# Weight tiles of one mode instead of two, with six of their real parts loaded as 40 and 24 rows

## The chip, the core and the metric

The kernel runs on one core of one Trainium2 chip. Its time is the device time of one execution, in microseconds (us), and the figure that is compared is the median over runs. The core has TensorE (PE), VectorE (DVE), ScalarE (ACT), GpSimd (POOL) and SyncE (SP), each with its own instruction order, and 16 DMA engines which the transfers of all queues share.

## The reference

Inputs are q, k, v of shape (8, 8, 576, 64) (batch, head, position, width), spectral weights `w_r` and `w_i` of shape (64, 512, 512) and `w_ch` of shape (512, 512), all fp32. The weights `w_r` and `w_i` are 64 MB of fp32 each.

```python
scores = (q @ k.transpose(0, 1, 3, 2)) / sqrt(64)
rel = pos[:, None] - pos[None, :]
local   = (rel >= 0) & (rel < 32)                       # heads 0 to 3
strided = (rel >= 0) & (pos[None] % 32 == pos[:, None] % 32)  # heads 4 to 7
x = softmax(where(mask, scores, -1e9)) @ v              # (8, 576, 512) over all heads
X = rfft(x, axis=1)[:, :64]                             # 64 modes
Yr = Xr @ w_r[m] - Xi @ w_i[m]                          # for each mode m
Yi = Xr @ w_i[m] + Xi @ w_r[m]
u = x + irfft(Y, n=576, axis=1)
out = u + relu(u @ w_ch)
```

## The kernel before

**Stages.** The order of work on every engine is written out by hand. First comes the strided attention (heads 4 to 7) batch by batch, a loop `for b in range(B)` in which the front work of the next batch (transposes of its q, k and v) is woven into the scores of this one; each batch ends with its share of the forward transform, so that the spectrum `Xh[1]` is complete after it. Then the local attention (heads 0 to 3) runs batch by batch, and between its steps lie the products of "slot 0": for all 64 modes, the half of the channels that the strided heads gave. `NMODES` says how many modes go with each batch. When the local heads are done, `Xh[0]` is complete and "slot 1" follows: for all 64 modes the other half of the channels. Between those modes lie other pieces from a list `work` (`w_turn`, which folds the inverse transform's turn into the channel weights, then `turn` and `premix` of each batch) and `spec`, which carries finished groups of 16 modes back; for the last ten modes of the loop (`LATE = 10`, modes 51 to 60) the list gives two pieces a mode. Modes 61 to 63 are done among the first steps of the tail. The tail adds the inverse transform's last group, takes the relu (`v_rows`), adds it to u (`u_rows`) and writes the output in 512 KB transfers.

**One mode.** `mode(slot, m)` does 16 matmuls (line 547) of a 128x128 piece of the weight tile with a 128x16 piece of the spectrum. The tile has the real part of the weights in partitions 0 to 63 and the imaginary part in 64 to 127, so one product sums both. Mode 0 has no imaginary part in its input and uses 64 partitions.

**Weights.** `w_fetch` (line 174) issues the loads of a tile on GpSimd's queue; the transfer turns fp32 into fp16, so an 8 KB row in DRAM becomes 4 KB in a partition. A tile holds two consecutive modes: 8 KB in each of 128 partitions. Its real part is one transfer of 64 partitions by two modes (line 196), 512 KB as written, and its imaginary part is another. The last four modes, and the imaginary part of the tiles with mode 0, go mode by mode (line 199), 256 KB each. Tiles come from a pool `pw` with five buffers (`NWBUF = 5`), apart from three pairs, `GUEST`, which lie in the places of the spectra `Y0`, `X0` and `YT` before these are needed. `mode` calls `w_fetch` after each odd mode, so that a buffer that has just been read is asked for again; the first stage fetches ahead:

```python
        w_fetch([2, 1, 1, 1, 1, 1, 0, 0][b])
```

which with one tile before the loop makes eight pairs, 16 modes.

**Inputs of the attention.** `load_str(b, nb)` brings v, q and k of the strided heads into `ring`, a store of 12 slots of 2048 fp16, three slots to a batch. A batch's input is 72 rows of 32 positions by 64: rows 0 to 63 are one transfer (for `nb == 2`, one transfer for the two batches of an even and odd pair), and rows 64 to 71 of both batches of a pair are one more transfer of eight rows by two (64 KB). `load_loc` brings the local heads' q, k and v, 128 rows each, 288 KB.

**Queue.** GpSimd issues all these in the order of the program, and waits ahead of an issue until the buffer is free and until the transfer eight places earlier has landed: there are eight semaphores for its transfers, used in turn. GpSimd's other work lies in the tail, where it adds x to the relu (line 905).

**Tiles of the tail.** `w_ch` has a place of its own in `big`. The relu's output `rl` takes two tags, `xT` and `rl`, with two buffers each in the pool `ptr`; the output tiles `osb` take slots of `pw`, free once the last weights have been used.

Of the kernel before, what the change touches and what calls it, by code (L numbers as in the profile page):

```python
# [10 lines left out]
FP = mybir.dt.float32  # L11
F16 = mybir.dt.float16
# [6 lines left out]
DM = 512  # L19
NM = 64  # L20
# [3 lines left out]
JG = [(0, 6), (6, 11), (11, 16)]  # L24
SCALE = float(1.0 / np.sqrt(D))
NEG = -30000.0
NWBUF = 5


def _host_consts():  # L30
# [49 lines left out]
def kernel(  # L80
# [10 lines left out]
    nc = tc.nc  # L91
# [3 lines left out]
    big = ctx.enter_context(tc.tile_pool(name="big", bufs=1))  # L95
# [5 lines left out]
    def psum_pools(**bufs):  # L101
        pctx.close()
        for n, c in bufs.items():
            pss[n] = pctx.enter_context(
                tc.tile_pool(name="ps_" + n, bufs=c, space=PSUM)
            )

    def psum(kind, half=False):
        if half:
            return pss[kind].tile([128, 1024], F16, tag=kind, name=kind)  # L110
        return pss[kind].tile([128, 512], FP, tag=kind, name=kind)
# [16 lines left out]
    def const_load(eng, *which):  # L128
        for n in which:
            eng.dma_start(cs[n][:, 0 : hosts[names.index(n)].shape[1]], drams[n])  # L130
# [13 lines left out]
    def spectra_tile(n):  # L144
        if n == "X0":
            Xh[0] = big.tile([128, 4, B, 2, NM], F16, tag=n, name=n)
        else:
            YS[n] = big.tile([128, 4, 4, 16, 16], F16, tag=n, name=n)

    xb = [px.tile([128, 11, 256], F16, tag="xb", name="xb") for _ in range(B)]  # L150

    pw = ctx.enter_context(tc.tile_pool(name="pw", bufs=NWBUF))
    actx = ctx.enter_context(ExitStack())
# [3 lines left out]
    ring = pat.tile([128, 12, 2048], F16, name="ring")  # L157
# [8 lines left out]

    GUEST = {1: "Y0", 2: "X0", 7: "YT"}
    w_tiles = []  # L170
    w_chs = {}
    w_ch = big.tile([128, 4, DM], F16, name="w_ch")

    def w_fetch(n=1):
        for _ in range(n):
            i = len(w_tiles)
            if i >= 2 * NM:
                return
            half, m = 1 - i // NM, i % NM
            if i // 2 in GUEST:  # L180
                wt = big.tile([128, 2, 4, DM], F16, tag=GUEST[i // 2], name="wt")
            else:
                wt = pw.tile([128, 2, 4, DM], F16, tag="w", name="wt")
            for ri, src in enumerate((moe_w_r, moe_w_i)):
                dst = wt[ds(64 * ri, 64)]
                rows = src[m : m + 2, ds(256 * half, 256), :].rearrange(
                    "m (p c) e -> p m (c e)", c=4
                )
                dst = dst.rearrange("p m c e -> p m (c e)")


                ones = range(2)
                if ri and not m:
                    ones = [1]
                elif i < 2 * NM - 4:
                    nc.gpsimd.dma_start(dst, rows)  # L196
                    continue
                for j in ones:
                    nc.gpsimd.dma_start(dst[:, j], rows[:, j])
            w_tiles.extend((wt[:, 0], wt[:, 1]))  # L200

    def w_ch_fetch():
        nc.gpsimd.dma_start(w_ch, moe_w_ch.rearrange("(c p) e -> p c e", p=128))
        w_chs["n"] = w_ch

# [3 lines left out]
    SRC = {2: v, 0: q, 1: k}  # L209
    SLOT = {2: 0, 0: 1, 1: 2}  # L210

    def str_in(b, vi):
        return ring[0:72, 3 * (b % 4) + SLOT[vi], :]
# [2 lines left out]
        t = ring[:, ds(2 * (b % 6), 2), :].rearrange("p n x -> p (n x)")  # L216
        return t[:, ds(1152 * vi, 1152)]

    def load_str(b, nb):
        for vi in (2, 0, 1):  # L220
            n = 3 * (b % 4) + SLOT[vi]
            two = ring[:, n : n + 4 : 3, :]
            src = SRC[vi][b - b % 2 : b - b % 2 + 2, 4:8].rearrange(
                "b h (c r) d -> (h c) b (r d)", r=32
            )
            if nb == 2:
                nc.gpsimd.dma_start(two[0:64], src[0:64])
            else:
                nc.gpsimd.dma_start(ring[0:64, n, :], src[0:64, b % 2])
            if b % 2 == 0:  # L230
                nc.gpsimd.dma_start(two[64:72], src[64:72])

    def load_loc(*bs):
        for b in bs:
            if b >= B:
                return
            for vi in (2, 0, 1):
                nc.gpsimd.dma_start(
                    loc_in(b, vi),
                    SRC[vi][b, 0:4].rearrange("h (cb i) d -> (h cb) (i d)", i=18),  # L240
                )
# [294 lines left out]
    def mode(slot, m):  # L536
        half = 1 - slot
        mi, mg = m % 8, m // 8
        if mi == 0:
            ypt[slot] = psum("y")  # L540
        yp = ypt[slot]
        yv = yp.rearrange("p (m e x) -> p m e x", m=8, e=4)
        wt = w_tiles[slot * NM + m]
        pr = ds(0, 128 if m else 64)
        for e in range(4):
            for c in range(4):
                nc.tensor.matmul(  # L547
                    yv[:, mi, e, :],
                    wt[pr, XC[c], ds(128 * e, 128)],
                    Xh[half][pr, c, :, :, m],  # L550
                    start=(c == 0),
                    stop=(c == 3),
                )
        if m % 2 and (slot or m // 2 not in GUEST):
            w_fetch()
        ends = {7: 8}
        if slot and mg == 7:
            ends = {5: 6, 7: 2}
        if mi in ends:
            n = ends[mi]  # L560
            m0 = mi + 1 - n
            part = (
                slice(None),
                slice(None),
                mg // 2,
                slice(None),
                ds(8 * (mg % 2) + m0, n),
            )
            src = yp.rearrange("p (m e x) -> p e x m", m=8, e=4)[:, :, :, ds(m0, n)]
            if slot == 0:  # L570
                if m == 7:
                    spectra_tile("Y0")
                nc.scalar.activation(out=YS["Y0"][part], in_=src, func=ACTF.Copy)
            else:
                nc.vector.tensor_tensor(
                    out=YS["YT"][part], in0=src, in1=YS["Y0"][part], op=AluOp.add
                )
# [117 lines left out]


    psum_pools(tp=3, sc=3, av=2)
    load_str(0, 1)
    const_load(nc.scalar, "cI", "cM6", "cM5", "cFs")
    load_str(1, 1)  # L700
    const_load(nc.sync, "cMl", "cFl", "cA")
    load_str(2, 2)
    w_fetch()

    def str_front(b):
        return [
            lambda: str_v(b, 0), lambda: str_v(b, 1),
            lambda: str_v(b, 2), lambda: str_q(b, 0),
            lambda: str_back(b, 0),
            lambda: str_back(b, 1), lambda: str_q(b, 1),  # L710
            lambda: str_k(b, 0),
            lambda: str_k(b, 1), lambda: str_k(b, 2),
        ]
# [29 lines left out]
                )  # L743
    SPLIT = [0, 2, 4, 5, 7, 8, 10]
    for b in range(B):
        if b in (1, 3):
            load_str(b + 3, 2)
        load_loc(*[(), (), (), (), (0,), (1, 2), (3,), (4, 5)][b])
        w_fetch([2, 1, 1, 1, 1, 1, 0, 0][b])
        front = str_front(b + 1) if b + 1 < B else loc_front(0)  # L750
        for t in range(6):
            str_scores(b, t)
            if b > 0:
                if t < 2:
                    str_values(b - 1, 4 + t)
                elif t == 2:
                    dft(b - 1, 1)
            if t >= 2:
                str_values(b, t - 2)
            for w in front[SPLIT[t] : SPLIT[t + 1]]:  # L760
                w()
        if b == 1:
            nc.vector.memset(PL[:, 0:PS0], 0.0)
# [10 lines left out]
    for b in range(B):  # L774
# [12 lines left out]
        n = 0  # L787
        nm = NMODES[b]
        for mi in range(nm):
# [3 lines left out]
            n = upto  # L793
# [5 lines left out]
    ptr = ctx.enter_context(tc.tile_pool(name="ptr", bufs=1))  # L799
# [37 lines left out]
    n = 0  # L837
# [3 lines left out]
    for m in range(NM - 3):  # L841
# [7 lines left out]
        n = upto  # L849
# [11 lines left out]
    held, vps, ups, rls, osbs = {}, {}, {}, {}, {}  # L861
# [24 lines left out]
    def v_early(i, bank=None):  # L886
        b, t = units[i]
        vps[i] = psum("v") if bank is None else bank
        v0 = v0s[b][:, t, :] if t < 4 else v0h[b // 2]
        nc.tensor.matmul(vps[i], idn, v0, start=True, stop=False)  # L890

    def v_rows(i):
        b, t = units[i]
        if i not in vps:
            v_early(i)
        vp = vps.pop(i)
        rows_of(b, t, vp, zzs, False)
        if t % 2 == 0:
            n = len(rls) // 2 % 2
            rl = ptr.tile([128, 2, 576], FP, tag="xT" if n else "rl", bufs=2, name="rl")  # L900
            rls[b, t] = rls[b, t + 1] = rl[:, :, 0:DM]
        rl = rls[b, t][:, t % 2, :]
        nc.scalar.activation(out=rl, in_=vp, func=ACTF.Relu)  # L903
        if pool_adds(b, t):
            nc.gpsimd.tensor_tensor(out=rl, in0=rl, in1=x_rows(b, t), op=AluOp.add)  # L905
# [56 lines left out]
    for i in range(len(units)):  # L962
        v_rows(i)
        b, t = units[i]
# [42 lines left out]
```

## Time and profile before

| | |
|---|---|
| median of 3 runs | 436.64 us (436.57 to 437.36) |
| the profiled execution | 436.57 us, of which 434.8 us are the span from the first to the last instruction |
| PE, DVE, ACT, POOL busy | 334.7, 215.0, 188.0, 129.3 us |
| DMA | 92.16 MB written by 28995 packets, mean 212 GB/s |
| mean granted TensorE clock | 0.821 of full speed |
| weight transfers | 122 of 512 KB, 10 of 256 KB |
| GpSimd's transfers in all | 184 |

A row of slices cuts the span into 40 equal stretches, and a digit is the busy share in tenths. A row of the stretches' view gives start and end, the length, then busy time and number of instructions of PE, PE's weight loads, DVE, ACT and POOL, the granted clock, the DMA engines' busy share and GB/s. The chain of waits is followed back from the last instruction, each step to what released it: a piece has its start, its length and what it was. A row of the issue view has the transfer, the queue, how many, KB each, and the median time in us from issue to landing. Names are those of the program, and L547 is line 547 of the kernel that is profiled; in the changed kernel line numbers are two or three lower in most of the file.

### The profile page before, as it was taken

How to read it: one execution, taken by the hardware profiler on the slowest of the kernel's cores; microseconds unless marked ns; L12 is line 12 of the kernel's file. 1: busy time of each engine (PE TensorE's matmuls, PEld its weight loads, DVE VectorE, ACT ScalarE, POOL GpSimd, SP SyncE). 2: the span in 40 equal slices, each digit the busy share in tenths (PEclk: the TensorE clock that was granted, in tenths of full speed). 3: DMA queues.
4: the chain of work that ended last, by engine and by line, in shares of the span. 5: the costliest groups of instructions: out<-in, count | busy, mean ns of one | idle time of the engine just before them, and what ended most of it. 6: DMA issues, size and time to landing. Idle time of an engine off the chain costs nothing.

```text
span 434.8 us, 12063 instructions
## 1 busy us (share of the span) xinstructions
PE 334.7 (77%) x5289; PEld 241.1 (55%) x5289; DVE 215.0 (49%) x466; ACT 188.0 (43%) x353; POOL 129.3 (30%) x208
## 2 busy tenths in 40 slices
PE   1987988789876879787865567679596769888994
PEld 1865776667765666665753345445454445554442
DVE  2788788744452242442511034244335443764895
ACT  1587678635542433534440302113313312443883
POOL 6423332323232222222222222222222222200893
PEclk9999899869895585988885559585769687999999
DMA  8999999999999999999999999999999999980787
GB/s 174 210 212 213 214 212 213 211 210 212 214 214 212 214 213 214 214 213 214 214 213 213 213 213 214 214 214 213 213 213 214 213 213 215 213 176 13 268 316 287
DMA packets 28995, 92.16 MB, mean 212 GB/s; under 512 B 4048, under 2 KB 5072, under 8 KB 28944
## 3 DMA queue, kind: packets, MB, share of 16 engines
q0 software_dynamic: 24704, 81.28, 94.2%
q1 hardware_dynamic: 3440, 9.46, 5.8%
q10 hardware_dynamic: 800, 0.67, 0.6%
q8 instruction: 41, 0.67, 0.6%
q14 instruction: 10, 0.08, 0.0%
HBM read 163.22 MB, written 9.44 MB: 397 GB/s over the span
## 4 chain that ended last, share of the span: by engine, by line
DMA 73%; PE 19%; DVE 2%; issue 2%; ACT 1%; POOL 1%; DVEq 0%; POOLq 0%
DMA wt<-in_moe_w_i_dram 51%; DMA ring<-in_v_dram 7%; DMA ring<-in_k_dram 6%; DMA wt<-in_moe_w_r_dram 4%; DMA ring<-in_q_dram 4%; PE sc L645 3%; PE y L547 3%; PE v L688 2%; PE u L688 2%; PE v L890 2%; PE y L514 1%; PE tp L653 1%; DVE yy L678 1%; PE u L911 1%; DVE xT L597 1%
## 5 line engine op out<-in xcount | busy, mean ns | idle before, releaser
L547 PE MATMUL y<-X,wt 128*128 128x16 f16 (+1 forms) x2048 | 82.4, 192 | 63.5 <-DMA wt<-in_moe_w_i_dram 60.9
L547 PEld LDWEIGHTS <-wt 128*128 128x128 f16 (+1 forms) x2048 | 72.6, 103 | 75.6 <-issue 72.3
L196 POOL DMA_DIRECT2D wt<-in_moe_w_r_dram x62 | 36.5, 589 | 142.2 <-PE y L547 63.1
L196 POOL DMA_DIRECT2D wt<-in_moe_w_i_dram x60 | 35.4, 590 | 70.6 <-DMA wt<-in_moe_w_i_dram 57.9
L654 ACT ACTIVATE v<-sc 128x512 f16<-128x512 f32 x32 | 18.9, 597 | 86.1 <-PE sc L645 86.0
L645 PE MATMUL sc<-w_cp,xT 128*128 128x512 f16 (+1 forms) x160 | 51.3, 450 | 0.4 <-DVE xT L617 0.4
L471 ACT ACTIVATE PL<-sc 128x480 f16<-128x480 f32 (+1 forms) x48 | 27.6, 579 | 47.4 <-PE sc L457 46.9
L655 DVE COPY xo<-tp 128x512 f16<-128x512 f16 x32 | 22.1, 692 | 45.5 <-PE tp L653 45.5
L250 DVE TENSOR_TENSOR xb<-av,rec 90x256 f16<-90x256 f32 (+2 forms) x80 | 36.0, 450 | 2.8
L249 DVE RECIPROCAL rec<-av 90x4 f32<-90x4 f32 (+2 forms) x80 | 14.7, 183 | 42.1 <-PE av L486 31.3
L402 DVE COPY qT<-tp 128x576 f16<-128x576 f16 x16 | 12.0, 758 | 42.8 <-PE tp L395 39.4
L260 ACT ACTIVATE v<-tp 128x640 f16<-128x640 f16 (+1 forms) x24 | 19.4, 808 | 21.2 <-PE tp L429 17.8
L395 PE MATMUL tp<-cI_s,ring 64*64 64x64 f16 x864 | 26.4, 210 | 2.2 <-issue 1.4
L360 ACT ACTIVATE PL<-sc 90x360 f16<-90x360 f32 (+1 forms) x48 | 22.7, 490 | 5.6 <-PE sc L353 4.9
L922 DVE TENSOR_TENSOR osb<-u,rl 128x512 f32<-128x512 f32 x36 | 23.6, 688 | 2.6 <-PE u L688 1.3
L395 PEld LDWEIGHTS <-ring 64*64 64x64 f16 x864 | 20.6, 122 | 7.4 <-issue 4.4
L905 POOL TENSOR_TENSOR rl<-rl,xo 128x512 f32<-128x512 f32 x16 | 18.3, 1156 | 20.5 <-ACT rl L903 20.2
L441 PE MATMUL sc<-cMl_s,cI_s 128*128 128x480 f16 (+1 forms) x48 | 22.4, 467 | 1.6 <-ACT X L260 1.6
L260 ACT ACTIVATE kz<-tp 64x360 f16<-64x360 f16 (+1 forms) x32 | 19.0, 595 | 10.2 <-PE tp L395 8.6
L457 PE MATMUL sc<-qT,kz 128*128 128x160 f16 (+1 forms) x160 | 22.6, 267 | 0.2 <-issue 0.2
L645 PEld LDWEIGHTS <-xT 128*128 128x128 f16 (+1 forms) x160 | 14.5, 109 | 14.6 <-issue 5.7
L285 PE MATMUL tp<-cI_s,ring 72*128 72x72 f16 x256 | 15.1, 206 | 9.5 <-DMA ring<-in_v_dram 8.0
(103 smaller groups left out, 647.8 us busy)
## 6 DMA issues: line engine op xcount, KB each, us to landing
wt<-in_moe_w_r_dram POOLq DMA_DIRECT2D x62, 512.0 KB, 18.9
wt<-in_moe_w_i_dram POOLq DMA_DIRECT2D x60, 512.0 KB, 19.4
out_dram<-osb SPq DMA_DIRECT2D x14, 512.0 KB, 2.7
ring<-in_v_dram POOLq DMA_DIRECT2D x8, 288.0 KB, 13.4
ring<-in_q_dram POOLq DMA_DIRECT2D x8, 288.0 KB, 13.6
ring<-in_k_dram POOLq DMA_DIRECT2D x8, 288.0 KB, 13.2
ring<-in_v_dram POOLq DMA_DIRECT2D x3, 512.0 KB, 15.5
ring<-in_q_dram POOLq DMA_DIRECT2D x3, 512.0 KB, 14.9
```

The costliest lines, as they stand in the source:

```text
L196: nc.gpsimd.dma_start(dst, rows)
L250: nc.vector.tensor_tensor(out=dst, in0=val.rearrange("p h (q c) -> p h c q", c=4), in1=rec[0:n, 0:pieces] .to_broadcast((n, pieces, 64)) . ...
L260: nc.scalar.activation(out=out, in_=in_, func=ACTF.Copy)
L360: nc.scalar.activation(out=PS[0:n, ds(POFF[t], 4 * n)], in_=scp[0:n, 0 : 4 * n], func=ACTF.Exp, scale=SCALE,)
L395: nc.tensor.transpose(tp[ds(64 * hp, 64), ds(64 * i, 64)], qn[ds(64 * hp, 64), ds(64 * (9 * g + i), 64)], idn[ds(64 * hp, 64), ds(64 * hp, ...
L441: nc.tensor.matmul(scp[:, 0 : n * times].rearrange("p (h x) -> p h x", h=times), idn, mask_rows("cMl", n, times), start=True, stop=False,)
L457: nc.tensor.matmul(scp[:, ds(col, n)], kzs[par][:, hp, ds(s0, 128)], qTs[par][:, ds(s0, n)], start=False, stop=(i == len(todo) - 1),)
L471: nc.scalar.activation(out=dst, in_=src, func=ACTF.Exp, scale=SCALE)
L547: nc.tensor.matmul(yv[:, mi, e, :], wt[pr, XC[c], ds(128 * e, 128)], Xh[half][pr, c, :, :, m], start=(c == 0), stop=(c == 3),)
L645: nc.tensor.matmul(vp[pr, :], xT[:, ch, cols], w_chs["cp"][:, ch, :], start=(ch == 0), stop=(ch == 3),)
L655: nc.vector.tensor_copy(out=xo[pr].rearrange("p (h q c) -> p h q c", h=2, c=4), in_=tp[pr, 0:512].rearrange("p (h c q) -> p h q c", h=2, c=4),
L922: nc.vector.tensor_tensor(out=osb[:, t % 2, :], in0=up, in1=rls[b, t][:, t % 2, :], op=AluOp.add)
```

## The change

A weight tile now holds one mode, 4 KB in a partition, and `pw` has eleven buffers. Each part of a tile is a transfer of its own with 64 rows, 256 KB. The six guest tiles use two halves each of the same three places. `mode` fetches after every mode, and the first stage fetches 17 modes ahead instead of 16. `w_ch` and `rl` take slots of `pw`.

`load_str(b)` loads the 64 rows of one batch only, and the loop calls it for one batch in each of its first five passes, not for two batches in two of them. The eight rows that are left of two batches remain one transfer.

Six tiles, i = 28, 45, 62, 79, 96 and 113 in the order of all 128 (`CUT`), have the real part loaded by two transfers, of 40 and of 24 rows.

Numbers of transfers on GpSimd's queue go from 184 to 321. The order of instructions on PE, VectorE, ScalarE and SyncE is unchanged.

```diff
-NWBUF = 5
+NWBUF = 11
...
-    GUEST = {1: "Y0", 2: "X0", 7: "YT"}
+    GUEST = {3: ("Y0", 0), 4: ("Y0", 1), 5: ("X0", 0), 6: ("X0", 1)}
+    GUEST |= {15: ("YT", 0), 16: ("YT", 1)}
+    CUT = range(28, 2 * NM, 17)
+    guests = {}
     w_tiles = []
     w_chs = {}
-    w_ch = big.tile([128, 4, DM], F16, name="w_ch")
...
-            if i // 2 in GUEST:
-                wt = big.tile([128, 2, 4, DM], F16, tag=GUEST[i // 2], name="wt")
+            if i in GUEST:
+                n, j = GUEST[i]
+                if j == 0:
+                    guests[n] = big.tile([128, 2, 4, DM], F16, tag=n, name="wt")
+                wt = guests[n][:, j]
             else:
-                wt = pw.tile([128, 2, 4, DM], F16, tag="w", name="wt")
-            for ri, src in enumerate((moe_w_r, moe_w_i)):
-                dst = wt[ds(64 * ri, 64)]
-                rows = src[m : m + 2, ds(256 * half, 256), :].rearrange(
-                    "m (p c) e -> p m (c e)", c=4
-                )
-                dst = dst.rearrange("p m c e -> p m (c e)")
-                ones = range(2)
-                if ri and not m:
-                    ones = [1]
-                elif i < 2 * NM - 4:
-                    nc.gpsimd.dma_start(dst, rows)
-                    continue
-                for j in ones:
-                    nc.gpsimd.dma_start(dst[:, j], rows[:, j])
-            w_tiles.extend((wt[:, 0], wt[:, 1]))
+                wt = pw.tile([128, 4, DM], F16, tag="w", name="wt")
+            for ri, src in enumerate([moe_w_r, moe_w_i] if m else [moe_w_r]):
+                rows = src[m, ds(256 * half, 256), :].rearrange("(p c) e -> p c e", c=4)
+                cuts = (0, 40, 64) if i in CUT and not ri else (0, 64)
+                for a, z in zip(cuts, cuts[1:]):
+                    nc.gpsimd.dma_start(wt[64 * ri + a : 64 * ri + z], rows[a:z])
+            w_tiles.append(wt)

     def w_ch_fetch():
+        w_ch = pw.tile([128, 4, DM], F16, tag="w", name="w_ch")
...
-    def load_str(b, nb):
+    def load_str(b):
         for vi in (2, 0, 1):
-            n = 3 * (b % 4) + SLOT[vi]
-            two = ring[:, n : n + 4 : 3, :]
-            src = SRC[vi][b - b % 2 : b - b % 2 + 2, 4:8].rearrange(
-                "b h (c r) d -> (h c) b (r d)", r=32
-            )
-            if nb == 2:
-                nc.gpsimd.dma_start(two[0:64], src[0:64])
-            else:
-                nc.gpsimd.dma_start(ring[0:64, n, :], src[0:64, b % 2])
+            nc.gpsimd.dma_start(
+                str_in(b, vi)[0:64],
+                SRC[vi][b, 4:8].rearrange("h (c r) d -> (h c) (r d)", r=32)[0:64],
+            )
             if b % 2 == 0:
-                nc.gpsimd.dma_start(two[64:72], src[64:72])
+                n = 3 * (b % 4) + SLOT[vi]
+                nc.gpsimd.dma_start(
+                    ring[64:72, n : n + 4 : 3, :],
+                    SRC[vi][b : b + 2, 4:8].rearrange(
+                        "b h (c r) d -> (h c) b (r d)", r=32
+                    )[64:72],
+                )
...
-        if m % 2 and (slot or m // 2 not in GUEST):
+        if slot or m not in GUEST:
             w_fetch()
...
-    load_str(0, 1)
+    load_str(0)
...
-    load_str(1, 1)
+    load_str(1)
...
-    load_str(2, 2)
-    w_fetch()
+    load_str(2)
+    w_fetch(2)
...
-        if b in (1, 3):
-            load_str(b + 3, 2)
+        if b < 5:
+            load_str(b + 3)
...
-        w_fetch([2, 1, 1, 1, 1, 1, 0, 0][b])
+        w_fetch([3, 3, 2, 2, 2, 1, 1, 1][b])
...
-            n = len(rls) // 2 % 2
-            rl = ptr.tile([128, 2, 576], FP, tag="xT" if n else "rl", bufs=2, name="rl")
-            rls[b, t] = rls[b, t + 1] = rl[:, :, 0:DM]
+            rls[b, t] = rls[b, t + 1] = pw.tile([128, 2, DM], FP, tag="w", name="rl")
```

## Prediction

> **What bounds the kernel now.** I read the page's slices first, then its queues and the chain, then stretches, and last the packet records engine by engine.
>
> ```profile
> DMA  8999999999999999999999999999999999980787
> q0 software_dynamic: 24704, 81.28, 94.2%
> DMA 73%; PE 19%; DVE 2%; issue 2%; ACT 1%; POOL 1%; DVEq 0%; POOLq 0%
> ```
>
> The 16 DMA engines are full from the first slice to about 385 us. One queue, GpSimd's, carries nearly all of it, and 73% of the chain that ended last is transfers. The stretches (busy time per engine; the last three columns are granted clock, DMA share and GB/s) give the limits by stage:
>
> ```profile
> 190.00:385.00 195.00, 142.65 (x2122) 98.54 (x2121) 76.04 (x157) 56.86 (x100) 46.26 (x79) 0.75 1.07 213
> 385.00:394.00 9.00, 7.83 (x94) 4.87 (x93) 5.27 (x11) 3.67 (x7) 0.00 (x0) 1.00 0.61 122
> 397.60:434.80 37.20, 31.26 (x148) 13.85 (x146) 27.63 (x46) 24.90 (x44) 22.79 (x20) 0.97 0.67 255
> ```
>
> Up to 385 us the stream is the limit (PE 73% busy, at a granted clock of 0.75); behind it PE is. Where one passes to the other, the chain of waits shows:
>
> ```profile
> 350.00 18.91 DMA wt<-in_moe_w_i_dram
> 368.91 0.14 issue
> 369.05 0.65 PE y L547 x16
> ...
> 373.90 0.12 issue
> 374.02 0.65 PE y L547 x16
> ```
>
> Weights of modes 52 and 53 land at 368.91, mode 52 starts 0.14 later, and that is the last landing on the chain. Mode 54 waits 0.12 more for its own pair; from there PE and VectorE work without a gap that a landing ends, modes finish at 397.6, and the tail runs to 434.8. So two things count: when weights of modes about 51 and 52 land, and how much PE work then lies ahead.
>
> Own time: 436.57 us = span 434.80 + 1.77 around it. The median of the three runs is 436.64, so I sum against 436.57 and correct nothing. A difference of 0.2%, 0.87 us, is about what a measurement of this kernel can tell from none.
>
> **Bytes do not change.** Every weight, q, k and v row is still read once, in rows of 8 KB (fp32) that land as 4 KB. PE, VectorE, ScalarE and SP keep their instruction order; only GpSimd's list of transfers changes, 184 to 321.
>
> **More transfers.** The issue view shows the old size and, where before already issues halves, the new one:
>
> ```profile
> wt<-in_moe_w_r_dram POOLq DMA_DIRECT2D x62, 512.0 KB, 18.9
> wt<-in_moe_w_i_dram POOLq DMA_DIRECT2D x60, 512.0 KB, 19.4
> wt<-in_moe_w_i_dram POOLq DMA_DIRECT2D x6, 256.0 KB, 13.5
> wt<-in_moe_w_r_dram POOLq DMA_DIRECT2D x4, 256.0 KB, 15.0
> ```
>
> In the packet records a 4096-byte row takes 304.7 ns of one engine, and each transfer ends with a 4-byte packet on every engine that takes 20.6 ns. A 64-row transfer puts 4 rows on each of 16 engines: 4 x 304.7 + 20.6 = 1239 ns; its two-mode form 8 x 304.7 + 20.6 = 2458 ns; both lengths stand between completions in the trace. Up to the landing of slot-1 mode 51 the changed kernel has issued 297 transfers against 168: 129 x 20.6 ns = 2.66 us on every engine, all on the path, since the engines are full. This is the one sure cost.
>
> The Trainium skill (DMA: Bandwidth & Descriptors, Rules for kernel authors) speaks against the change: it wants transfers of 1 MiB or more, since each costs about 2.0 us beside its bytes. Taken serially 129 x 2.0 = 258 us would be added, an estimate by that page; the row above, 20.6 ns with eight outstanding, holds here, because completions of this queue overlap the next transfers' rows.
>
> **Issue.** GpSimd spends 0.52 to 0.60 us on one issue. Two or three per mode are at most 1.8 us against 2 x 1.239 = 2.48 us of stream. It only ever waits, on this path, for the transfer eight earlier or for a buffer:
>
> ```profile
> POOL wt L196 <- DMA wt<-in_moe_w_i_dram: 66.4, 43, 2.7
> POOL wt L196 <- PE y L547: 63.1, 23, 6.0
> ```
>
> Eight outstanding transfers of half the size are 9.9 us of stream in place of 19.7. From landing to the next issue's first row I read 0.28 to 0.53 (wait), 0.52 (issue) and 0.93, some 2 us; a late engine still has 7 x 1.239 = 8.7 us queued. So I cost the shorter queue at nothing, hidden by those 8.7 us. Were the cover gone, it would cost up to 2 us each time. The buffers cover it too: eleven single tiles instead of five pairs, so a tile needs the mode ten or eleven before it, about 25 us earlier, and PE lags a landing by at most 6.5 us (mode 61). GpSimd's later adds (line 905) come behind its last issue. In the first stage, b-loop transfers move (one batch's 64 rows each pass), but their ring slots come free 10 us or more ahead; zero. `w_ch` and the tail's `rl` now take slots of the weight pool some ten allocations apart; zero, and the 37.2 us tail stays.
>
> **Finer landing.** An even mode no longer waits for its partner: it lands half a pair, 2.458 us, earlier. Mode 52 would land at 368.91 - 2.46 + 2.66 = 369.11. Mode 51 however landed with its pair at 364.05 and now lands at 364.05 + 2.66 = 366.71, starts at 366.85, and the trace has 2.78 us of PE work from a start of 51 to 52 without the wait. So 52 starts at 369.63 instead of 369.05, 0.58 late. Of that 0.28 goes into the wait ahead of mode 54 (the 0.12 idle, plus a matmul overlap of 0.16 that the records show whenever nothing is waited for). The rest, **+0.3 us**, reaches the end. So of 2.66 us of completions, 2.36 are given back by the granularity.
>
> **The cut.** This is the open term. The 16 engines are not equal: completion packets of one transfer spread over 1.1 us early on and 6.4 us at the end (eight engines finish the last transfer within 2.1 us, eight 5.4 to 6.4 us later). The late eight are those that also fetch PE's program:
>
> ```profile
> q8 instruction: 41, 0.67, 0.6%
> ```
>
> Each fetch takes 0.9 to 1.0 us of one engine, in turn over the same eight. A landing needs the slowest engine, so how six cuts distribute rows decides. Before shows neither 40 nor 24 rows; its nearest rows are the eight-row transfers (two batches, 16 rows), which go to only eight engines, and successive ones to alternate halves. By them 40 rows are 5 on one half and 24 are 3 on the other: one row more and one less per cut, six times, 6 x 304.7 ns = 1.83 us. Twelve eight-row transfers precede the first cut, so its 40 rows fall on the half that got the first of them. Of the late engines two lie in that half, six in the other. Upper end: the two get 1.83 us more, and landings are +1.83. Lower end: no late engine gets more and all are relieved, -1.83. If rows are dealt over more engines and the start rotates, the effect is nearer zero. The nearest row says +1.83, but only if 40 and 24 are dealt like 8; I take half of it, **+0.9 us**, keeping -1.83 and +1.83 as ends.
>
> The Trainium skill (DMA: Bandwidth & Descriptors, Why a DMA increments its semaphore by 16 and not by 1) says rows go to the largest number up to 16 that divides them, from a rotating start: 40 as 10 x 4, 24 as 12 x 2. Worked through six cuts this is +2 rows on four engines, -2 on four: 0 to +0.6 us, an estimate by that page that would make the time 436.9 to 437.5; no transfer of before can show it.
>
> **Sum.** 436.57 + 0.3 + 0.9 = 437.8 us.
>
> **Rivals.**
> - **The cut relieves all late engines** (faster). Its place is the eight engines that fetch PE's program; price 6 x 304.7 ns. It decides if the 40 rows fall on none of them: landings move by 2.66 - 1.83, mode 51 still leads, and the end is 0.3 - 1.83 = -1.5: 435.0 us. For it: the spread of 6.4 us is large enough to be relieved. Against it: two late engines lie in the other half.
> - **The half pair at the end gives nothing back**, because other work holds PE as long as the landing did, or slow engines spread even and odd landings: all 2.66 us and the cut's 0.9 arrive: 440.1 us. Against it: PE starts 0.14 after a landing at nearly every pair before.
> - **The shorter queue runs dry.** 66.4 us of GpSimd's waits are for a transfer eight earlier; if the earliest engine empties while the latest holds the semaphore back (spread 6.4 of 9.9 us), re-issue shows on the fast engines, and on all when it passes 8.7 us. Some 2 us in a few places: 441 to 445 us. Against it: before's half-size transfers near the end landed after 13.5 us, with no gap in the late engines' packets.
> - **The change does nothing by this measure**: cut near zero, 436.57 + 0.3 = 436.9. It is the low end of my own case.
>
> **How the numbers follow.** Forecast case 0.62, own range 436.9 (cut at 0) to 438.7 (cut at +1.83); relieved engines 0.18; no gain at the end 0.10; queue runs dry 0.05; 0.05 for what I don't see. The range reaches from the relieved case, 434.9, to the case without the gain, 440.3; a relieved engine gains its six rows at most, so most of that case lies inside; left out are the dry queue, the unseen and the far sides of the two bounding cases, together under 0.2. Faster by over 0.2% (under 435.7): the relieved case and a little of the unseen, 0.20. Within 0.2% (435.7 to 437.4): the forecast case with the cut under +0.6, some 0.38 of it, 0.24. Slower: the rest, 0.56.
>
> **What would show it.** Right: weight transfers 256 KB with 20.6 ns completions; modes 51 and 52 starting some 0.14 us behind landings near 367.7 and 370.1; tail 37.2 us. The cut's share shows in the spread of one transfer's completions over the 16 engines: over 6.4 us at the end if it adds to late engines, near 4.6 if it relieves them. Wrong: gaps between packets on the late engines in 20 to 380 us, GpSimd's waits for `y` naming a tile that a mode still holds, or a tail that is longer.

## The result: 0.8% slower, three times the forecast loss

The changed kernel takes 440.49 us in the median of four runs (439.76 to 441.05), the kernel before 436.88 us on the same chip. The ratio is 1.0081, with a 95% interval of 1.006 to 1.0101. Forecast were 437.8 us and a range up to 440.3, so the sign was right and the size was not. The profiled execution took 440.10 us against 436.57, which is 3.53 us more.

From the page of the changed kernel, the 40 slices, GpSimd's queue and PE's program fetches, and the chain by engine:

```profile
DMA  9999999999999999999999999999999999991687
q0 software_dynamic: 26992, 81.29, 94.6%
q8 instruction: 42, 0.69, 0.6%
DMA 50%; PE 32%; DVE 10%; issue 3%; ACT 2%; POOL 1%; DVEq 0%; POOLq 0%
```

The stream now fills its slices up to about 394 us, where before the slice from 380 to 391 us was no longer full; its last transfer lands at 398.87 us in place of 393.77. (The chain's share of DMA falls from 73% to 50%, though in the first stretch below the engines are as busy as before; I take it that with finer landings more pieces of the chain are PE's.) The same stretches as before, each moved along with the modes:

```profile
190.00:387.50 197.50, 142.14 (x2101) 96.64 (x2098) 75.76 (x156) 56.24 (x100) 82.41 (x160) 0.75 1.06 209
387.50:396.60 9.10, 7.93 (x95) 4.94 (x94) 5.38 (x11) 3.77 (x7) 1.03 (x2) 1.00 0.90 179
400.20:438.20 38.00, 31.28 (x149) 13.84 (x146) 27.62 (x46) 24.89 (x44) 22.77 (x20) 0.98 0.66 250
```

Two readings follow. The stream moves 209 GB/s where it moved 213, at nearly the same DMA share (1.06 against 1.07). And the tail is 38.00 us long instead of 37.20, though all five columns are busy as long as before: PE 31.28 us against 31.26. The 0.80 us lie in its last stretch, before and after:

```profile
427.60:434.80 7.20, 1.62 (x8) 0.53 (x6) 2.58 (x5) 0.91 (x2) 0.69 (x1) 0.87 0.70 258
430.20:438.20 8.00, 1.64 (x8) 0.55 (x6) 2.59 (x5) 0.92 (x2) 0.70 (x1) 0.89 0.64 237
```

The issue view (KB each, then median us from issue to landing) shows the new transfers and the cut ones:

```profile
wt<-in_moe_w_i_dram POOLq DMA_DIRECT2D x126, 256.0 KB, 9.6
wt<-in_moe_w_r_dram POOLq DMA_DIRECT2D x122, 256.0 KB, 9.4
wt<-in_moe_w_r_dram POOLq DMA_DIRECT2D x6, 160.0 KB, 9.7
wt<-in_moe_w_r_dram POOLq DMA_DIRECT2D x6, 96.0 KB, 9.3
```

Where stream and PE meet, the chain of waits now reads (start, length, what):

```profile
351.01 10.45 DMA wt<-in_moe_w_i_dram
361.46 0.14 issue
361.60 0.65 PE y L546 x16
362.25 1.71 PE sc L644 x4
...
369.42 0.87 PE sc L644 x4
```

The last landing on the chain is mode 48's at 361.46. In this execution PE ran at half its clock behind it (four products take 1.71 us at 362 and 0.87 at 369; the granted clock over 350 to 370 us is 0.66), so from there it is PE by a hair: mode 51 lands at 368.55 and starts at 368.77, 0.22 behind. Mode 52 starts at 371.65 against 369.05 before, 2.60 us later; the last mode starts 2.61 later; PE's last matmul of the tail ends 2.61 later; the span ends 3.44 later. So 2.61 us were lost up to mode 52, 0.82 behind PE's last matmul, 0.10 outside the span (1.87 against 1.77).

### The profile page after: what moved, and what is told of

Read it like the earlier page. It is cut to its first block, busy times and chain, and to the rows that moved or that the text cites. A ratio compares the mean times of both kernels' runs of the same rounds, so it can differ in the third digit from the quotient of the medians.

```text
span 438.2 us, 12336 instructions
## 1 busy us (share of the span) xinstructions
PE 337.5 (77%) x5289; PEld 242.5 (55%) x5289; DVE 216.0 (49%) x466; ACT 188.5 (43%) x353; POOL 189.9 (43%) x345
## 4 chain that ended last, share of the span: by engine, by line
DMA 50%; PE 32%; DVE 10%; issue 3%; ACT 2%; POOL 1%; DVEq 0%; POOLq 0%
DMA wt<-in_moe_w_i_dram 35%; DMA wt<-in_moe_w_r_dram 13%; PE y L546 4%; PE sc L644 4%; DVE kz L291 2%; PE sc L513 2%; DVE xb L249 2%; PE u L687 2%; PE v L687 2%; PE v L889 2%; DMA ring<-in_q_dram 2%; PE sc L352 1%; PE tp L323 1%; PE tp L394 1%; PE sc L344 1%
## 5 line engine op out<-in xcount | busy, mean ns | idle before, releaser
L196 POOL DMA_DIRECT2D wt<-in_moe_w_r_dram x134 | 69.0, 515 | 123.7 <-DMA wt<-in_moe_w_r_dram 27.2
L196 POOL DMA_DIRECT2D wt<-in_moe_w_i_dram x126 | 64.9, 515 | 63.4 <-DMA wt<-in_moe_w_i_dram 39.1
L394 PE MATMUL tp<-cI_s,ring 64*64 64x64 f16 x864 | 25.1, 207 | 1.7 <-DVE kz L401 0.9
L900 ACT ACTIVATE rl<-v 128x512 f32<-128x512 f32 x36 | 20.4, 597 | 4.2 <-PE v L687 3.5
```

Source lines behind the costliest of these rows:

```text
L196: nc.gpsimd.dma_start(wt[64 * ri + a : 64 * ri + z], rows[a:z])
L394: nc.tensor.transpose(tp[ds(64 * hp, 64), ds(64 * i, 64)], qn[ds(64 * hp, 64), ds(64 * (9 * g + i), 64)], idn[ds(64 * hp, 64), ds(64 * hp, ...
```

## Experiments

In the sets of runs the median of the kernel before lay between 437.3 and 437.7 us, so ratios to it are what is compared. "Mode 51" is the landing of its weights in the profile. By "even share" I mean the time at which a transfer would complete if all 16 engines had equal work, from the packet times in the prediction; "late" engines are counted against it at the last transfer, and these figures are good to about 0.3 us. A landing is that of one profiled execution: the same list of transfers landed mode 51 at 368.55 (changed kernel) and 369.27 us (e8_less_pool), and at 364.18 (e7) and 364.79 (e9). So single landings differ by up to 0.7 us for no reason in the program.

| run | ratio to before, 95% interval | mode 51, us | late engines at the last transfer |
|---|---|---|---|
| before | | 364.05 (pair) | eight, at 4.1 to 5.0 us |
| changed kernel | 1.0081 (1.006 to 1.0101) | 368.55 | five, at 6.5 to 7.2 |
| e1_no_cut | 1.0012 (0.9998 to 1.0026) | 366.92 | eight, at 4.3 to 5.0 |
| e2_32_32 | 1.0023 (1.0009 to 1.0038) | 367.11 | eight, at 3.9 to 5.0 |
| e3_13_cuts | 1.0117 (1.010 to 1.0133) | 370.60 | five, at 8.3 to 9.1 |
| e4_24_first | 1.0055 (1.0038 to 1.0073) | 368.55 | five, at 5.5 to 6.4 |
| e5_pair_tiles_single_loads | 1.0006 (0.9994 to 1.0019) | 366.88 | eight, at 4.1 to 5.9 |
| e7_last16_single | 0.9976 (0.9961 to 0.9991) | 364.18 | eight, at 3.7 to 4.8 |
| e9_last16_less_pool | 0.9937 (0.9912 to 0.9962) | 364.79 | |

### The cut taken away, made even, made more frequent

Three edits of one line of the changed kernel:

```diff
 # e1_no_cut
-                cuts = (0, 40, 64) if i in CUT and not ri else (0, 64)
+                cuts = (0, 64)
 # e2_32_32
-                cuts = (0, 40, 64) if i in CUT and not ri else (0, 64)
+                cuts = (0, 32, 64) if i in CUT and not ri else (0, 64)
 # e3_13_cuts
-    CUT = range(28, 2 * NM, 17)
+    CUT = range(28, 2 * NM, 8)
```

> The changed kernel with every part as one transfer of 64 rows (no cut). Half-and-half theory (a cut's 40 rows give eight engines one row more each, its 24 rows give the other eight one row less, always the same eight): weights of slot-1 mode 51 land 1.83 + 0.10 us earlier than in the changed kernel's profile, at 366.6 us, and the time falls by 1.7 to 2.1 us, to about 438.5 (ratio to before 1.003 to 1.005). Rotating theory (40 rows as 10 engines by 4, 24 as 12 by 2, from a start that moves): at most 0.7 us less, 439.8. Count theory (what was lost is the number of transfers, each dearer than 20.6 ns): 0.1 to 0.3 us less, 440.2.

> The changed kernel with the six parts cut into 32 and 32 rows in place of 40 and 24: the same 321 transfers, and by every theory of dealing the same rows on each engine. Half-and-half theory: as without a cut plus 6 x 20.6 ns, mode 51 lands at 366.7, about 438.6 us. Rotating theory: 0 to 0.6 us below the changed kernel, 439.9. Count theory: the changed kernel's 440.5 unchanged.

> The changed kernel with 13 parts cut into 40 and 24 rows in place of six (every eighth tile from the 28th). Half-and-half theory: seven more rows on the late engines of one half, 7 x 304.7 ns = 2.1 us, plus 7 x 20.6 ns: mode 51 lands near 370.5 us, about 442.5 us. Rotating theory: worked through 13 cuts two engines have two rows more and two have two less, so within 0.3 us of the changed kernel. Count theory: 0.1 to 0.4 us more, 440.8.

The chain of waits of e1_no_cut around mode 51, which now waits for its own landing as the prediction's steps had it (366.71):

```profile
357.29 9.63 DMA wt<-in_moe_w_i_dram
366.92 0.14 issue
367.06 0.65 PE y L546 x16
```

that of e2_32_32:

```profile
358.71 8.41 DMA wt<-in_moe_w_i_dram
367.11 0.05 issue
367.16 0.66 PE y L546 x16
```

and that of e3_13_cuts:

```profile
360.97 9.63 DMA wt<-in_moe_w_i_dram
370.60 0.14 issue
370.74 0.65 PE y L546 x16
```

Without a cut mode 51 lands 1.62 us earlier, with 32 and 32 rows 1.44 earlier at the same 321 transfers, and with 13 cuts 2.05 later. (That hit on the expected 370.5 is partly luck: the expectation counted seven more cuts, but only five of them lie ahead of mode 51, which makes 1.63 us.) With eleven cuts ahead of mode 51 the landing has moved by 3.68 us against none, 0.33 per cut on average (0.27 over the first six, 0.41 over the other five): one row of 304.7 ns and one completion of 20.6. Rotating dealing (0 to 0.7 us in all) and dear transfers (e2 like the changed kernel) are refuted. It is the unequal rows that cost, one per cut on the late engines. In time e1 came out better than expected, 1.0012 for 1.003 to 1.005; 0.50 us of that is a shorter end of the program (the drain, below), which the expectation did not count.

### Which engines get the row: 24 first, and the first load cut

```diff
 # e4_24_first
-                cuts = (0, 40, 64) if i in CUT and not ri else (0, 64)
+                cuts = (0, 24, 64) if i in CUT and not ri else (0, 64)
```

> The changed kernel with the same six parts cut into 24 rows first and 40 second. Half-and-half theory: the other eight engines now get the row more. In the changed kernel five of the late engines ended at 6.5 to 7.2 us behind the even share and three had fallen among the others; here three end that late and five have fallen; mode 51 still lands 1.4 us later than with 32 and 32 rows, near 368.5 us, about 440 us. Rotating theory: the same engines as with 40 first, no more than 0.6 us from the uncut kernel. If the order of the two transfers decided through their issue and not through rows, the changed kernel's five would stay the late ones.

Mode 51 lands at 368.55 as with 40 first, and again five engines end late and three have fallen. Alternate halves would have shown three late. So the half-and-half dealing, with which I had taken the size of the ends, is wrong, and as many of the late engines get the row in either order. How rows are dealt was then read from one transfer on an empty queue:

```diff
 # e11_first_load_cut, no cut in the weights
...
+            cuts = (0, 40, 64) if (b, vi) == (0, 2) else (0, 64)
...
```

> The changed kernel without cuts in the weights, but with the very first transfer (64 rows of v, queue empty) split into 40 and 24 rows: the 16 completion times of the 40-row transfer show how rows are dealt, since an engine without rows completes 3 x 304.7 = 0.9 us or more ahead of one with three. Rounded-up dealing (three rows on each of 13 engines, one on the 14th, none on two): two or three early completions. Half-and-half: eight early ones and eight at 5 x 304.7 ns. Divisor dealing (ten engines by four): six early ones.

The 16 completion times of the 40-row transfer and then of the 24-row one, in us from the span's start, sorted:

```
40 rows: 4.14 4.23 | 4.52 | 4.90 4.92 4.94 5.00 5.02 5.15 5.16 5.17 5.21 5.25 5.27 5.43 5.69
24 rows: 4.82 4.86 5.24 | 5.97 6.06 6.14 6.21 6.22 6.23 6.27 6.27 6.28 6.47 6.50 6.63 6.85
```

Two engines complete at once, one about 0.3 us later, thirteen from 0.7 us later on: three rows on each of 13 engines, one on the 14th, none on two. With the 24 rows three engines complete early again; a fourth without rows would still have its three rows of the first transfer to finish and cannot be told from the rest. That is rounding up: 40/16 is 3 rows, 24/16 is 2 rows on 12 engines. Together twelve engines get five rows where an even transfer gives four, one gets three, one gets one, two get none. This was one load of v; the weights' own cuts show it by their number of packets. An engine's empty place is filled by a packet of four bytes (in this run two engines run three such packets within 12 ns, at 3.41 and at 3.60 us), and the pages count packets under 512 bytes, here of e1_no_cut, e2_32_32 and the changed kernel:

```profile
DMA packets 31094, 92.20 MB, mean 212 GB/s; under 512 B 6144, under 2 KB 7168, under 8 KB 31040
DMA packets 31190, 92.20 MB, mean 211 GB/s; under 512 B 6240, under 2 KB 7264, under 8 KB 31136
DMA packets 31286, 92.20 MB, mean 210 GB/s; under 512 B 6336, under 2 KB 7360, under 8 KB 31232
```

From the first to the second come 96, the 16 completions of six more transfers. From the second to the third, with as many transfers, come 96 again, 16 per cut: the 8 empty places of 3 x 16 for 40 rows and the 8 of 2 x 16 for 24. Ten engines by four and twelve by two would leave 32. So six cuts are +6 rows, 1.83 us, on twelve engines in both orders. The trace does not name an engine, but as five stay late, five of the eight that also fetch PE's program would be among the twelve. The Trainium skill (DMA: Bandwidth & Descriptors, Why a DMA increments its semaphore by 16 and not by 1) has this too, as an exception on trn2 for some direct copies of GpSimd's queue; I had used its general rule of divisors.

### Transfers and tiles apart; cuts without short queues

```diff
 # e5: before, but every mode's part its own transfer, mode by mode
-                elif i < 2 * NM - 4:
-                    nc.gpsimd.dma_start(dst, rows)
...
+            parts = [(0, 2)] if False else [(0, 1), (1, 2)]
+            for a, z in parts:
+                for ri, src in enumerate((moe_w_r, moe_w_i)):
...
+                    nc.gpsimd.dma_start(dst[:, a1:z], rows)
 # e6: before, three pair tiles cut
-                    nc.gpsimd.dma_start(dst, rows)
+                    cuts = (0, 40, 64) if i in (28, 62, 96) and not ri else (0, 64)
+                    for a, z in zip(cuts, cuts[1:]):
+                        nc.gpsimd.dma_start(dst[a:z], rows[a:z])
```

> The kernel before with its pair tiles and its five buffers, but every part of every mode a transfer of its own (first both parts of the even mode, then of the odd one): the number of weight transfers and the finer landing alone, without cuts. My sum: 2.6 us of completion packets, 2.3 of it given back because an even mode lands half a pair earlier, so 0.3 us over before, 437.0; mode 51 lands near 366.6. Count theory: as late as the changed kernel, 440. A theory that the loss lies in the tiles and buffers rather than in the transfers: as before, 436.6, or below.

> The kernel before with the real parts of three of its pair tiles (modes 28 and 62 of slot 0's and slot 1's count: tiles 28, 62 and 96 with their partners) loaded as 40 and 24 rows, each of two modes: as many rows moved as by six cuts, nothing else changed. Half-and-half theory: 6 x 304.7 ns on the late engines, modes 52 and 53 land at 370.7 instead of 368.9, about 1.8 us over before (ratio 1.004). Theory that a cut hurts only with short queues of half-size transfers: no change from before, 1.000.

e5 is 1.0006 of before: twice as many transfers, and no loss that can be measured; mode 51 lands at 366.88 where 366.71 was worked out. So completions cost what I took, and the half pair gives them back. e1_no_cut, which has the new tiles and buffers and the moved loads of the first stage besides, is at 1.0012, so these cost nothing that can be told either. The profiled run of e5 profiled run, the slowest of 13 with 441.18 us, had PE at a granted clock of 0.89 from 370 to 400 us (0.94 in those of e3, e6 and e8, 1.00 in the others), so only its landings are read. e6 does not bear out what was expected: its ratio is 1.001, interval 0.9985 to 1.0034, so no change lies inside and the expected 1.004 just outside. In its profile, one of the slower of its runs (440.17 us, median 438.20), modes 52 and 53 land at 371.07 against 368.91, and four late engines stand at 6.2 to 6.6, four at 3.9 to 4.9. Its edit also does not move the rows that were meant. The packets of before and of e6:

```profile
DMA packets 28995, 92.16 MB, mean 212 GB/s; under 512 B 4048, under 2 KB 5072, under 8 KB 28944
DMA packets 29235, 92.16 MB, mean 210 GB/s; under 512 B 4288, under 2 KB 5312, under 8 KB 29184
```

Of 240 more, 48 are completions of three transfers and 192 fill empty places, 64 per cut. Rounding up, with two rows to a partition, would leave 32. Ten engines by eight rows (six times eight places empty) and twelve by four (four times four) leave 64. So by this count two-mode transfers of 40 and 24 are dealt by divisors, and e6 says nothing of the changed kernel's cuts. Why its landing comes 2.16 us later stays open.

### The tail: GpSimd's closing drain

The trace has one instruction that the profile's page does not count as busy: a drain with which GpSimd ends its program. It begins as the last add does (line 905, in the changed kernel 902), and in all rows of the table but the last 0.79 us after its end the span is over:

| run | transfers in all | of them since GpSimd's last long stop | drain, us | from PE's last matmul to the end, us |
|---|---|---|---|---|
| before | 184 | 62 | 6.92 | 5.58 |
| e1_no_cut | 315 | 66 | 7.24 | 5.90 |
| changed kernel | 321 | 72 | 7.74 | 6.40 |
| e7_last16_single | 196 | 74 | 7.90 | 6.56 |
| e3_13_cuts | 328 | 79 | 8.31 | 6.96 |
| e8_less_pool | 321 | 72 | 7.73 | 5.13 |

The drain grows by 0.082 us per transfer ((8.31 - 6.92)/17) since the last "long stop", a pause of 3.1 to 3.5 us with every semaphore already there, which GpSimd makes ahead of its transfer 122 or 123 (counted from 0) with pair transfers, ahead of 128 and 249 in the changed kernel and its variants. In before the drain ended only 0.16 us behind SyncE's last wait; in the changed kernel 0.77. To test that the drain ends the program, its start was moved:

```diff
 # e8_less_pool (changed kernel), e9 (e7), e10 (before): one add fewer on GpSimd
-        if (b, t) in ((0, 1), (B - 1, 3)):
+        if (b, t) in ((0, 1), (B - 1, 3), (B - 1, 4)):
```

> The changed kernel with the relu's last add on GpSimd (batch 7, tile 4) given to PE as one more matmul of 0.22 us, as the program does for other tiles. Drain theory (GpSimd's closing drain, 7.74 us from its last add, ends the program in the changed kernel 0.77 us behind SyncE's last wait): the drain starts 1.5 us earlier or more and no longer ends last; from PE's last matmul to the end 5.6 to 5.8 us in place of 6.4, so 0.4 us less in all after the extra matmul. If the drain only waits for something else that ends late, the 6.4 us stay.

From PE's last matmul to the end 5.13 us in place of 6.40, with the drain as long as before (7.73) but begun 3.6 us ahead of PE's last matmul instead of 2.1. The drain now ends 1.04 us ahead of the end, so something else ends last; e9 and e10 have the same 5.13 us. Expected were 5.6 to 5.8 us. In time the ratio is 1.0044 (1.0026 to 1.0062); the changed kernel's 1.0081 (1.006 to 1.0101) is of another set and the intervals touch, so the profile shows this gain more surely than the times.

### A version that beats both

What was found points to finer landing only where it is used, and a shorter end.

```diff
 # e7: before, parts mode by mode from slot-1 mode 48 on
...
+            parts = [(0, 2)] if i < 2 * NM - 16 else [(0, 1), (1, 2)]
...
```

> The kernel before with single-mode transfers for the last 16 modes of slot 1 only (12 transfers more than before): the finer landing where PE meets the stream, without the completion packets of the other 112 tiles. My steps: mode 51 then binds as it lands with its half at about 364.1, mode 52 starts near 367.1 in place of 369.05, the last mode 2.3 us earlier. The closing drain of GpSimd grows by about 12 x 0.08 = 1.0 us (it was 6.9 us with 62 transfers since GpSimd's last long stop, 7.2 with 66, 7.7 with 72, 8.3 with 79) and gives back 0.8 of it: 435.1 against 436.6, ratio 0.9965. If the half pair is not what counts: 436.9 or above.

> The kernel before with single-mode transfers for the last 16 modes and, besides, the relu's last add (batch 7, tile 4) taken from GpSimd and given to PE. In the run with the 16 modes alone 6.56 us lay between PE's last matmul and the end (5.58 before), since GpSimd's drain had grown to 7.9 us. Drain theory: the drain starts 1.5 us earlier against PE, 5.3 us are left, and 0.22 us go to the extra matmul: 1.0 us under the run with the 16 modes alone, about 435.0 (ratio 0.995). If something else ends there: 0.998, as with the 16 modes alone.

> The kernel before with only that last add given to PE. Its drain ended 0.16 us behind SyncE's last wait, so by the drain theory at most a few tenths are to be had: tail from PE's last matmul to the end 5.1 to 5.4 us in place of 5.58, 0.22 us more of PE work: 436.4 to 436.7, ratio 0.999 to 1.001. If the add on GpSimd itself was late for the output: 0.997 or below.

e7 is faster than before: 0.9976, interval 0.9961 to 0.9991. Mode 51 lands at 364.18 with its own half, mode 52 starts at 367.30 and the last mode 1.79 us earlier than before (2.3 expected), of which the drain takes 0.98. With the add moved as well, e9 is at 0.9937 (0.9912 to 0.9962), 435.13 us against 437.65. The add alone, e10, gives 0.9989 (0.9977 to 1.0002), as the drain theory had it: before's tail had little to win.

## Why the prediction was off, by its own steps

| step | forecast, us | measured, us |
|---|---|---|
| completions less the half pair | +0.3 | +0.75 (e1's last mode 397.70 against 396.95) |
| the cut | +0.9, ends -1.83 and +1.83 | +1.87 (last mode 399.56 against e1's 397.70) |
| tail and closing | 0 | +0.82 |
| outside the span | 0 | +0.10 |
| sum | +1.2 | +3.53 |

**The cut** is the term that was mis-sized. I worked out +1.83, then took half of it because the trace of before showed neither 40 nor 24 rows. The upper end was about right (1.87 by the last mode, 1.62 by the landing of mode 51), through a dealing that was wrong: not half and half but rounded up, +1 on twelve engines. That the upper end fits is partly luck: the dealing that was assumed happened to move one row per cut as well. The cost came out surely because whoever gives twelve of 16 engines a row more hits at least four of the eight late ones, in any order.

**The tail** is the step that failed. "The 37.2 us tail stays" looked at engines that are counted as busy. The closing drain is no busy time, and a chain followed back from the last instruction to PE's does not name it; yet in before it already ended last, by 0.16 us, and so nothing stood between ten more transfers (62 to 72 since the last long stop) and the end: 0.82 us.

**Completions and the finer landing** held: 20.6 ns each, mode 51 within about 0.2 us of the step in e1 and e5. Too low was the rest, by 0.45 us: in e1 mode 52 starts 0.88 us late where 0.58 was worked out, and 0.75 reach the last mode, so the wait ahead of mode 54 took up 0.13 us and not the 0.28 that I let vanish there; in the changed kernel mode 52 is 2.60 and the last mode 2.61 us late, and it took up nothing. The sign that I named for mode 52, a start 0.14 us behind its landing, did not go with this step, by which it starts 2.78 us after mode 51; it started 0.60 us behind its landing at 371.05.

**The rivals.** "The half pair gives nothing back" named 440.1 us, the time of the profiled run to the tenth, and is wrong: e5 and e1 show the half pair paid back. A time that fits does not show its reason. "The cut relieves all late engines" is wrong by its sign: mode 51 lands at 368.55 with the cuts and at 366.92 without. (Its sum gives 436.57 + 0.3 - 1.83 = 435.0, while the range starts at 434.9; nothing hangs on that.) **The shorter queue** did make early engines run dry, as that rival said they would show first, but not the late ones. GpSimd waits in changed places:

```profile
POOL wt L196 <- DMA wt<-in_moe_w_i_dram: 58.3, 94, 1.6
POOL wt L196 <- DMA wt<-in_moe_w_r_dram: 43.5, 55, 1.9
...
POOL wt L196 <- PE y L546: 12.8, 11, 3.9
```

It waits longest, 3.9 us, at a long stop (ahead of transfer 249; the engine named had long been done: the buffer that it needed was free 16 us earlier). The stop cost the earliest engine 1.1 us and the latest nothing, and a landing asks only for the latest. It did spoil one of my tests: I meant to tell relief from burden by the spread of a transfer's completions, over 6.4 us if the cut adds, near 4.6 if it relieves. It was 4.2 while the cut added; I take it that with 9.9 us outstanding early engines cannot run further ahead, as it was 6.4 us with 19.7. The lateness against the even share, 7.2 us instead of 5.0, is what should have been named.

## What to carry to other kernels

On a saturated stream a landing comes from the latest engine, so an extra row there is paid in full. For loads with one row to a partition on this queue, count rows per engine by rounding up, and keep the partitions a multiple of 16 (32 + 32 rows cost 0.2 us of landing over no cut, 40 + 24 cost 1.6) unless the uneven share is known to go where it helps. With two rows to a partition the dealing was another one, so count the packets before relying on it. Twice as many transfers cost almost nothing here once they land finer where PE waits for them, so make them finer only there. Before writing that a tail stays, look for what ends last behind the last busy instruction, each engine's closing drain included.

## What was not expected of the hardware

GpSimd pauses for 3.1 to 3.5 us with nothing to wait for, ahead of one of its transfers 122 to 128 (counted from 0) and, where there are that many, 121 transfers later again; and its drain at the end costs 0.082 us per transfer since then (6.51 us for 57 in e5, 8.31 for 79). What it does in either was not settled; a common count of transfers that it must tidy up would fit both. PE's granted clock near the end goes with single runs that are some us longer: from 370 to 400 us it was 0.89 in e5's slowest run (441.18 us, median 437.82) and 0.94 in the profiled runs of e3, e6 and e8, which lie 1.0 to 2.0 us above their medians.
